# One mixing step for three head groups in the first layer of a decode kernel

## The chip, the core and the metric

The kernel runs on one core of a Trainium2 chip. The metric is the device time of one execution in microseconds; the figure for a kernel is the median of its runs. Beside those times there is one profiled execution, whose trace gives the span (first to last instruction) and every instruction and transfer in it.

## The reference

Two layers, the same weights and caches in both. Each layer is an attention block over a cached sequence of 8192 positions, for one new position in each of 4 batches, followed by a gated feed-forward block; both have a layer norm before them and are added to x.

```python
def A(x, k_cache, v_cache, wq, wo):        # x: 4 x 1 x 512, caches: 4 x 8 x 8192 x 128
    q = (x @ wq).reshape(B, Sq, 32, 128).transpose(0, 2, 1, 3)
    k, v = repeat(k_cache, 4, axis=1), repeat(v_cache, 4, axis=1)
    p = softmax(einsum("bhqd,bhkd->bhqk", q, k) * 128 ** -0.5)
    o = einsum("bhqk,bhkd->bhqd", p, v)
    return o.transpose(0, 2, 1, 3).reshape(B, Sq, 4096) @ wo
def B(x, w_gate, w_up, w_down):            # 512 -> 1792 -> 512
    return (silu(x @ w_gate) * (x @ w_up)) @ w_down
x = x + A(layernorm(x), ...)
x = x + B(layernorm(x), ...)
x = x + A(layernorm(x), ...)
x = x + B(layernorm(x), ...)
```

All tensors are bfloat16. The two caches are 268 MB together if each were read once for each layer (part of what layer 1 has loaded last is kept for layer 2).

## The kernel before, in words

**Units and groups.** The 8 key/value heads make 4 groups `gp` of two heads, each group with 8 query heads (`H2`). With 4 batches there are 16 units `u` = 4 gp + b. A unit has one K block and one V block of 4 MB (4096 KB, 128 partitions x 32 KB). In the text, K13 and V13 are the blocks of unit 13. Layer 1 (`L` = 0 in the code) goes through the groups in the order 0, 1, 2, 3, layer 2 through 3, 0, 1, 2.

**Slots and transfers.** Blocks lie in four slots of one large tile `kvf`, and a fifth place that wq holds at first. All loads are issued by SyncE (SP) in one order that the program writes out (`cmds`). Each waits until the room that it writes is free; `freed` marks a room free, and `pump` issues whatever can then be issued, in order. After the last V blocks of layer 1 come the weights of the feed-forward block: gate and up into the slot of V13, then two parts of `w_down`, and then three more parts of `w_down`, each written over a quarter of the gate weights as soon as the products with that quarter (line 1016) have read it. Behind them come K blocks of layer 2, each into room that the feed-forward block gives back.

**One unit.** VectorE (DVE) transposes the K block in place (`turn`, line 567), two of its eight parts at a time. TensorE (PE) makes the scores from each part (`scores`, line 593, four products of 512 columns for a part). Then come a maximum (lines 599, 604, 607), the exponential on ScalarE (ACT, line 641), a transpose of the weights p (`turn_p`, line 659), the products with V (line 731, 16 for each half), the gathering of the heads' outputs out of PSUM on DVE (`gather`, lines 779 and 783), and a small product with `sel` and a scaling (`combine`, lines 788 and 793) that put the unit's eight heads into the tile `oT`.

**The end of a group.** When the four batches of a group are done, `close_group` queues what follows. `mix` (line 815) rearranges the group's columns of `oT` by 16 small products into PSUM and one copy back (line 819), since `w_o` was loaded with four rows beside one another on a partition. `rows` (line 850) then makes 8 products for the group, each with 4 columns of `oT` as weights and 512 columns of `w_o` moving; all groups but the last add up in one PSUM bank. When the last but one group of a layer is in, `upright` turns the 4 x 512 sum into the layout of x: four times a copy on ACT (line 864) and a small transpose on PE (line 860), and then an addition to x on DVE (line 804). The last group goes another way (`out_proj`, line 875), directly in the layout of x.

**What sets the order.** The instruction order of each engine is fixed when the program is built. Score and value work is held in a list `blocks`, each with 0.9 us; small steps stand in a list `line`, each with the time that should pass before it. Running a block advances `line` by the block's time, and due steps are emitted. `flush` empties `line` at once. It is called, among other places, in `finished` (line 536), when part 6 of K13 in layer 1 is done:

```python
if it == half_kept and a >= NB - 2:
    flush()
    hold(a, False)
```

`hold` (line 533) transposes the last two of the eight parts of K13 into PSUM, to keep them for layer 2; after that the slot of K13 is free. A second list, `later`, holds work for the end of the next unit's values.

In layer 1 the mixing of groups 0 and 1 is done when group 1 closes (`spot` gives a group's place in its layer's order), with their rows at the end of the next unit; group 2 is mixed and added when it closes. In layer 2 the first three groups are mixed together when the third closes.

Of the kernel before, what the change touches and what calls it, by code (L numbers as in the profile page):

```python
# [103 lines left out]
def bass_interleave_layers__gqa_block_cached__swiglu_ffn__decode_kernel(  # L104
# [40 lines left out]
    with ExitStack() as es:  # L145
# [35 lines left out]
        def pick2(k):  # L181
            o = k // 2 * 2 * P + k % 2
            return slice(o, o + 2 * P - 1, 2)
# [69 lines left out]
        n = FO * B  # L253
# [24 lines left out]
        def bank(k):  # L278
            return ps[:, k * BANKF:(k + 1) * BANKF]
# [75 lines left out]
        groups = [[0, 1, 2, 3], [3, 0, 1, 2]]  # L355

        def spot(L, gp):
            return groups[L].index(gp)
# [51 lines left out]
        n = NB - PARK  # L410
# [140 lines left out]
        line = []  # L551
# [162 lines left out]
        def values(L, u):  # L714
# [22 lines left out]
            def part(i):  # L737
# [18 lines left out]
                if i == 3:  # L756
                    more = later.pop(0)() if later else []
                    if p_name == "late":
                        freed(W_SLOT[L], NB, NB + 1)
                    if (L, u) == (0, NP - 2):  # L760
                        freed(W_SLOT[L], NB + 1, NB + 2)
                    done.add((L, u))
                    if last:
                        gather([QH - 1], ok3)
                        combine()
                    else:
                        line[0:0] = [[0.0, None, lambda: gather(range(QH), ok, True)], [1.3, None, combine]]
                    line.extend(behind.pop(u, []))
                    if all((L, gp * B + k) in done for k in range(B)):
                        close_group(L, gp, fill)  # L770
                    line.extend(more)
# [31 lines left out]
        def add_to_x(at, name):  # L803
            T.op("dve", lambda e: e.tensor_tensor(xT[:], xT[:], at, ALU.add), reads=["x", name], writes=["x"])  # L804

        def mix(L, gs, fill):
            C = len(gs) * H2 // NA
            mixed.update(gs)
            at, name = place("mix", 0, NA * C * B)
            names = [OT[g] for g in gs]  # L810
            now = oT[:, spot(L, gs[0]) * H2:(spot(L, gs[-1]) + 1) * H2]
            o = now.rearrange("p (c a) b -> p a c b", a=NA)
            for j in range(NA):
                for a in range(NA):
                    T.op("pe", lambda e: e.matmul(at[a * QB:(a + 1) * QB, j * C * B:(j + 1) * C * B],
                                                  lhsT=ident[:, j::NA], rhs=o[:, a], start=True, stop=True),
                         reads=["ident"] + names, writes=[name], sig=(j == NA - 1 and a == NA - 1))
            fill(1)
            T.op("dve", lambda e: e.tensor_copy(now.rearrange("p (c j) b -> p j c b", j=NA),  # L819
                                                at.rearrange("p (j c b) -> p j c b", j=NA, c=C)),  # L820
                 reads=[name], writes=names)

        mixed, later = set(), []

        def close_group(L, gp, fill):
            if gp == groups[L][-1]:
                line.extend([[0.5, None, lambda: mix(L, [gp], fill)], [0.7, None, lambda: out_proj(L, gp, fill)]])
                return
            n = spot(L, gp)
            if n < (1, 2)[L]:  # L830
                return
            gs = groups[L][:n + 1] if n == (1, 2)[L] else [gp]
            line.append([0.5, None, lambda: mix(L, gs, fill)])
            turned_back = upright() if gp == groups[L][-2] else []

            def in_rows():
                while gp not in mixed:
                    line.pop(0)[2]()
                for g in gs:
                    rows(L, g)  # L840
                return turned_back
            if turned_back and not L:
                line.extend([[0.7, None, in_rows]] + turned_back)
            else:
                later.append(in_rows)

        def rows(L, gp):
            for r in range(H2):
                h, o = gp * H2 + r, spot(L, gp) * H2 + r
                T.op("pe", lambda e: e.matmul(bank(OUTB)[0:B, 0:D], lhsT=oT[:, o, :], rhs=wo_sb[:, h, :],  # L850
                                              start=(gp == groups[L][0] and r == 0),
                                              stop=(gp == groups[L][GP - 2] and r == H2 - 1)),
                     reads=[f"wo{gp}", OT[gp]], writes=[f"pb{OUTB}"], sig=(r == H2 - 1))

        def upright():
            at, name = bank(LNB)[:, 4 * P - XB:4 * P], f"pb{LNB}"

            def step(kt):
                if kt:
                    T.op("pe", lambda e: e.matmul(at[:, (kt - 1) * B:kt * B], lhsT=row, rhs=identf[0:B, 0:B],  # L860
                                                  is_transpose=True, start=True, stop=True),
                         reads=["row", "ident"], writes=[name])
                if kt < KT:
                    T.op("act", lambda e: e.activation(row, bank(OUTB)[0:B, pick2(kt)], ACTF.Copy),
                         reads=[f"pb{OUTB}"], writes=["row", "pb"])
                else:
                    add_to_x(at, name)
            return [[0.9, None, lambda kt=kt: step(kt)] for kt in range(KT + 1)]
# [11 lines left out]
        def out_proj(L, gp, fill):  # L880
            project(L, gp)
            fill(1)
            add_to_x(*place("out", 0, XB))
# [268 lines left out]
```

## Time and profile before

| | |
|---|---|
| median of 3 runs | 644.83 us (644.80 to 645.44) |
| the profiled execution | 645.2 us, its span 642.9 us |
| busy: PE, PE weight loads, DVE, ACT | 413.0, 173.2, 424.9, 50.2 us |
| moved | 271.8 MB, mean 423 GB/s |
| row products (line 850) | 48 of them, 10.8 us busy |
| mixing products (line 815) | 80 of them, 1.2 us busy |
| mean granted clock of PE | 0.834 |

How to read it: the share of busy time is an average over the whole span. In the trace a line of the timeline gives start, length, engine, line of the code, operation, output and input, the number of instructions, and in brackets how long the engine was idle before and what ended that. Lines with SPq are issues of transfers, not the transfers. A line of the windows gives, for a stretch of the span, its length, the busy time and the number of instructions of PE, PE's weight loads, DVE, ACT and POOL, then PE's granted clock (1.00 is full speed), the share of the 16 DMA engines that was busy, and GB/s. A clock of 0.50 is half speed.

### The profile page before, as it was taken

To read this page: it belongs to the slowest core of one execution; us is meant where nothing else is said; L and a number is where in the kernel's file an instruction comes from. 1 tells how busy PE (TensorE), PEld (TensorE's weight loads), DVE (VectorE), ACT (ScalarE), POOL (GpSimd) and SP (SyncE) were. 2 spreads that over 40 slices of the span, in tenths; PEclk is the share of its full clock that TensorE was granted. 3 is DMA by queue.
4 is the path that set the end of the run, shared out by engine and by line. 5 is a ranking of instruction groups with operands and counts; after the bars stand their busy time and mean duration, and the time that the engine had idled before them with its cause. 6 is when DMAs were issued, how large, how long until landed. Compare 5 with 4: busy or idle time off the path is not lost.

```text
span 642.9 us, 6981 instructions
## 1 busy us (share of the span) xinstructions
PE 413.0 (64%) x2886; PEld 173.2 (27%) x2888; DVE 424.9 (66%) x597; ACT 50.2 (8%) x138; POOL 11.9 (2%) x44
## 2 busy tenths in 40 slices
PE   0583476457755757757866977667655477558766
PEld 0231122122222312222325332222222122223224
DVE  5375467456776656776953888977765567656953
ACT  0100000000000000000010300000000000000110
POOL 0000000000000000000000000000000000000000
PEclk9995886688876898768975899998767987679987
DMA  9999999999999999999999999999999999999996
GB/s 365 451 423 414 436 430 432 433 428 423 436 438 427 426 432 433 433 430 429 428 414 386 416 435 431 433 431 429 434 428 430 435 430 432 424 436 429 431 414 261
DMA packets 16014, 271.76 MB, mean 423 GB/s; under 512 B 1640, under 2 KB 1648, under 8 KB 7536
## 3 DMA queue, kind: packets, MB, share of 16 engines
q1 hardware_dynamic: 15984, 271.33, 99.1%
q8 instruction: 22, 0.36, 0.2%
q14 instruction: 8, 0.07, 0.0%
HBM read 271.32 MB, written 0.00 MB: 422 GB/s over the span
## 4 chain that ended last, share of the span: by engine, by line
DMA 60%; DVE 19%; PE 16%; issue 4%; ACT 0%; SPq 0%; POOL 0%; ACTq 0%; DVEq 0%; POOLq 0%
DMA kvf<-in_A_k_cache_dram 45%; DVE kvf L567 14%; DMA kvf<-in_A_v_cache_dram 11%; PE ps L593 10%; DMA kvf<-in_A_wq_dram 3%; PE ps L731 2%; DVE pb L783 2%; DMA kvf<-in_B_w_down_dram 1%; PE ps L982 1%; PE ps L1016 1%; DVE pT L659 1%; DVE pb L779 0%; DVE ps L533 0%; DVE scr L793 0%; PE ps L875 0%
## 5 line engine op out<-in xcount | busy, mean ns | idle before, releaser
L593 PE MATMUL ps<-kvf,zq 128*128 128x512 bf16 x1024 | 291.8, 431 | 185.6 <-DVE kvf L567 178.6
L567 DVE STREAM_TRANSPOSE kvf<-kvf 128x2048 f32<-128x2048 f32 (+1 forms) x133 | 280.5, 2132 | 125.5 <-DMA kvf<-in_A_k_cache_dram 125.3
L593 PEld LDWEIGHTS ps<-kvf,zq 128*128 128x128 bf16 x1024 | 98.9, 108 | 343.1 <-DVE kvf L567 222.6
L731 PE MATMUL ps<-kvf,pT 128*32 128x512 bf16 x960 | 65.8, 396 | 1.4 <-DVE pT L659 1.4
L641 ACT ACTIVATE pb<-ps,tiny 128x512 bf16<-128x512 f32 x32 | 24.9, 777 | 507.8 <-DVE tiny L639 507.8
L659 DVE STREAM_TRANSPOSE pT<-pb 64x512 bf16<-64x512 bf16 x60 | 41.2, 686 | 3.0 <-ACT pb L641 2.0
L783 DVE SCALAR_TENSOR_TENSOR pb<-ps,tiny,pb 128x128 f32<-128x128 f32 x104 | 36.5, 351 | 5.1 <-PE ps L731 1.4
L599 DVE TENSOR_REDUCE tiny<-ps 128x1 f32<-128x512 f32 x32 | 22.0, 688 | 20.5 <-PE ps L593 20.5
L731 PEld LDWEIGHTS ps<-kvf,pT 128*32 128x32 bf16 x960 | 20.8, 98 | 31.1 <-issue 15.4
L788 PEld LDWEIGHTS ps<-sel,pb 128*128 128x128 f32 x64 | 16.5, 266 | 16.4 <-DVE pb L783 8.0
L583 POOL TENSOR_TENSOR zq<-scr,tiny 128x64 bf16<-128x64 bf16 x30 | 9.2, 307 | 525.9 <-PE ps L593 525.9
L607 DVE TENSOR_REDUCE mrm<-ps 1x8 f32<-1x128 f32 x32 | 8.7, 273 | 13.5 <-PE ps L604 13.5
L788 PE MATMUL ps<-sel,pb 128*128 128x8 f32 x64 | 12.1, 262 | 5.4 <-DVE pb L783 5.4
L631 PEld LDWEIGHTS ps<-mrm,tiny 128*128 128x128 f32 x60 | 13.0, 223 | 9.3 <-issue 5.9
L982 PE MATMUL ps<-kvf,xn 128*4 128x512 bf16 x64 | 7.5, 621 | 11.2 <-DMA kvf<-in_A_wq_dram 10.9
L631 PE MATMUL ps<-mrm,tiny 128*128 128x16 f32 x60 | 10.0, 243 | 3.3 <-ACT mrm L644 3.3
L779 DVE TENSOR_SCALAR pb<-ps,tiny 128x128 f32<-128x128 f32 x32 | 10.1, 316 | 2.6 <-PE ps L731 2.6
L850 PE MATMUL ps<-wo_sb,scr 128*4 128x512 bf16 x48 | 10.8, 379 | 0.4 <-DVE scr L819 0.4
L644 ACT ACTIVATE mrm<-head,tiny 128x8 f32<-128x8 f32 x32 | 9.6, 301 | 1.0
L604 PE MATMUL ps<-identf,tiny 128*1 128x128 f32 x32 | 8.6, 270 | 1.2 <-DVE tiny L599 1.2
L804 DVE TENSOR_TENSOR xT<-xT,ps 128x16 f32<-128x16 f32 x6 | 1.0, 172 | 10.6 <-PE ps L860 4.7
L793 DVE TENSOR_TENSOR scr<-ps,rl 128x8 bf16<-128x8 f32 x32 | 5.7, 177 | 3.1 <-PE ps L788 2.1
(88 smaller groups left out, 122.6 us busy)
## 6 DMA issues: line engine op xcount, KB each, us to landing
kvf<-in_A_k_cache_dram SPq DMA_DIRECT2D x27, 4096.0 KB, 31.2
kvf<-in_A_v_cache_dram SPq DMA_DIRECT2D x27, 4096.0 KB, 33.8
kvf<-in_A_v_cache_dram SPq DMA_DIRECT2D x3, 2048.0 KB, 25.0
kvf<-in_A_k_cache_dram SPq DMA_DIRECT2D x11, 512.0 KB, 6.9
kvf<-in_A_k_cache_dram SPq DMA_DIRECT2D x2, 2048.0 KB, 9.4
kvf<-in_A_wq_dram SPq DMA_DIRECT2D x2, 2048.0 KB, 18.1
wo_sb<-in_A_wo_dram SPq DMA_DIRECT2D x4, 1024.0 KB, 41.5
kvf<-in_B_w_gate_dram SPq DMA_DIRECT2D x2, 1792.0 KB, 24.0
```

What stands on the lines that cost most here:

```text
L567: T.op("dve", lambda e: e.transpose(w, w), reads=names, writes=names)
L593: T.op("pe", lambda e: e.matmul(bank(bk)[:, 0:SW], lhsT=zq[:, z0:z0 + P], rhs=w[:, :, c // 2, :, c % 2], start=(q == 0 and c == 0), stop=( ...
L599: T.op("dve", lambda e: e.tensor_reduce(mx[:], bank(bk)[:, 0:SW], AX.X, ALU.max), reads=[f"pb{bk}"], writes=["mx"])
L631: T.op("pe", lambda e: e.matmul(at, lhsT=ones, rhs=mrm[:, i * H2:(i + 2) * H2], start=True, stop=True), reads=[f"m8{i}", "rsm", "onesf"], ...
L641: T.op("act", lambda e: e.activation(pb[:], bank(bk)[:, 0:SW], ACTF.Exp, bias=nm, scale=rstd[:, b:b + 1], accum_out=rs), reads=[f"pb{bk}", ...
L659: T.op("dve", lambda e: e.transpose(dst, pb[hp]), reads=["pb", "row"], writes=[name])
L731: T.op("pe", lambda e: e.matmul(bank(k)[j * QB:(j + 1) * QB, q0 * Dh:q1 * Dh], lhsT=p_t[:, t, h, :], rhs=v[:, q0:q1, t, :], start=((last o ...
L779: T.op("dve", lambda e: e.tensor_scalar(into, o, own[:, q:q + 1], None, op0=ALU.mult), reads=[f"pb{k}", "own"], writes=["row"] if last els ...
L783: T.op("dve", lambda e: e.scalar_tensor_tensor(into, o, own[:, q:q + 1], into, op0=ALU.mult, op1=ALU.add), reads=[f"pb{k}", "own", iname], ...
L788: T.op("pe", lambda e: e.matmul(at, lhsT=into, rhs=sel[:], start=True, stop=True), reads=[iname, "sel"], writes=[name])
L850: T.op("pe", lambda e: e.matmul(bank(OUTB)[0:B, 0:D], lhsT=oT[:, o, :], rhs=wo_sb[:, h, :], start=(gp == groups[L][0] and r == 0), stop=(g ...
L982: T.op("pe", lambda e: e.matmul(bank(QK[k])[a * QB:a * QB + B, :], lhsT=xn[:, kt * B:(kt + 1) * B], rhs=wq_sb[:, kt, f:f + W2], start=(kt ...
```

## The change

In layer 1, `close_group` now does nothing when groups 0 and 1 close. When group 2 closes, one `mix` takes the 24 heads of groups 0, 1 and 2 together: 16 small products of 24 columns instead of 16 of 16 columns and 16 of 8, and one copy instead of two. The 8 row products of each of the three groups are put into `line` as three steps with times of 0.7, 1.8 and 1.8 us, followed by the steps of `upright`. The number of row products is the same, 24 in each layer. Layer 2 is as before.

```diff
@@ close_group
             if gp == groups[L][-1]:
                 line.extend([[0.5, None, lambda: mix(L, [gp], fill)], [0.7, None, lambda: out_proj(L, gp, fill)]])
                 return
-            n = spot(L, gp)
-            if n < (1, 2)[L]:
+            if gp != groups[L][-2]:
                 return
-            gs = groups[L][:n + 1] if n == (1, 2)[L] else [gp]
+            gs = groups[L][:-1]
             line.append([0.5, None, lambda: mix(L, gs, fill)])
-            turned_back = upright() if gp == groups[L][-2] else []
+            turned_back = upright()
 
             def in_rows():
                 while gp not in mixed:
...
                 for g in gs:
                     rows(L, g)
                 return turned_back
-            if turned_back and not L:
-                line.extend([[0.7, None, in_rows]] + turned_back)
-            else:
+            if L:
                 later.append(in_rows)
+            else:
+                line.extend([[0.7 if g == gs[0] else 1.8, None, lambda g=g: rows(L, g)] for g in gs] + turned_back)
```

## The prediction

> **What bounds the kernel now.** I read the page first. Its part 2 says that the transfers never rest:
>
> ```profile
> DMA  9999999999999999999999999999999999999996
> GB/s 365 451 423 414 436 430 432 433 428 423 436 438 427 426 432 433 433 430 429 428 414 386 416 435 431 433 431 429 434 428 430 435 430 432 424 436 429 431 414 261
> ```
>
> The second line counts. 271.3 MB at the usual 431 GB/s is 629 us of a 642.9 us span. One place in the middle is slow: slice 22 (337.5 to 353.6 us), with 386 GB/s. It loses 16.07 x (1 - 386/431) = 1.7 us. It is the feed-forward part of the first layer, so I asked for SP's own timeline there:
>
> ```profile
> 296.97 14.30 SPq L93 DMA_DIRECT2D kvf<-in_A_v_cache_dram  x5
> 323.57 0.38 SPq L93 DMA_DIRECT2D kvf<-in_B_w_gate_dram  x1
> 324.00 2.14 SPq L93 DMA_DIRECT2D kvf<-in_B_w_up_dram  x3
> 338.42 0.33 SPq L93 DMA_DIRECT2D kvf<-in_B_w_down_dram  x1
> 338.80 0.41 SPq L93 DMA_DIRECT2D pT<-in_B_w_down_dram  x1
> 343.31 1.61 SPq L93 DMA_DIRECT2D kvf<-in_B_w_down_dram  x3
> ```
>
> The reader is to see how much is queued ahead of each issue. From 296.97 to 323.57 a loss is impossible: at 296.97 the last K block (4.19 MB, 9.7 us) is still to come, and at 323.57 some 5 MB of V are (11.5 us, bytes issued less bytes of the packets ended). At 343.31 it is different. The last V packets end at 334.7 us; behind them are only gate 1.835, up 1.835 and two quarter-megabyte parts of down, together 4.19 MB. At the 409 to 410 GB/s of 338 to 342 us they last 10.2 us, until 344.9. The next issue, 343.31, waits until the first gate products (L1016) have read the room it overwrites, and packets follow an issue by a little over 1 us here (the first issue is at 0.74, the first packets are in the stretch 1.5 to 2.0). So the queue is on the edge, and the windows of half a microsecond show it:
>
> ```profile
> 343.00:343.50 0.50, 0.50 (x22) 0.50 (x20) 0.01 (x1) 0.00 (x0) 0.00 (x0) 0.50 1.08 399
> 343.50:344.00 0.50, 0.50 (x11) 0.50 (x9) 0.00 (x0) 0.00 (x0) 0.00 (x0) 0.50 0.72 279
> 344.00:344.50 0.50, 0.50 (x20) 0.50 (x20) 0.00 (x0) 0.35 (x2) 0.00 (x0) 0.50 0.89 295
> 344.50:345.00 0.50, 0.50 (x22) 0.50 (x20) 0.03 (x1) 0.21 (x1) 0.00 (x0) 0.50 0.91 266
> ```
>
> The last two columns are the DMA share and GB/s: 280 in the mean of the last three lines against 410, so some 0.5 us is lost already. The slack here is nil. Whatever makes the first gate product later makes this hole longer, and the hole is not made good, because the DMA engines are busy from there to 639 us.
>
> **The change, part by part.** Units are (group, batch); K13 is the K block of unit 13.
>
> *Taken away at 210 and 214 us* (group 1 closes): 16 mixing products of 0.42 us together, one copy of 0.22 us (L819, 211.85), and 16 row products that take 3.62 us from 214.53. After them PE waits 3.46 us for the transpose of a K block, itself waiting for its DMA at 219.24. The transfer issued at 212.62, just behind the mixing, comes up to 0.42 us earlier, with 15 us queued ahead of it. Gain at the end: nothing, and covered so deeply that no bound is needed.
>
> *One mix of three groups instead of one group.* Layer 2 of this kernel already does just this: 16 products of 24 columns in 0.42 us (580.74), the same as the 16 of 8 columns at 288.45, and its copy takes 0.26 instead of 0.19. Cost +0.07 us.
>
> *The rows moved.* The list gives the three sets of rows due times of 0.7, 1.8 and 1.8, which looks like a spreading. The order of the changed kernel's instructions shows none: on PE all 24 row products stand in one block, just where the 8 stand now. The reason is in `finished`: when quarter 6 of K13's eight parts is done, `flush()` empties the whole list before `hold` puts the last parts of K13 into PSUM. In the trace this is the place:
>
> ```profile
> 288.45 0.42 PE L815 MATMUL ps<-scr,identf 128*32 128x8 bf16 x16
> 289.91 0.19 DVE L819 CAST scr<-ps 128x32 bf16<-128x32 f32 x1
> 290.25 1.89 PE L850 MATMUL ps<-wo_sb,scr 128*4 128x512 bf16 x8 [0.40 <-DVE scr L819]
> 294.48 0.17 DVE L804 TENSOR_TENSOR xT<-xT,ps 128x16 f32<-128x16 f32 x1 [4.38 <-PE ps L860]
> 298.07 2.29 DVE L567 STREAM_TRANSPOSE kvf<-kvf 128x2048 f32<-128x2048 f32 x1
> ```
>
> After the rows come four copies on ACT and four small products on PE in turn (L864, L860), the add to x, the two transposes of `hold`, a maximum, and only then K14's first transpose. DVE sits idle 4.38 us in this already and is in order, so K14's transposes stand behind it; so do the last quarter of K13 and V12 on PE. The price of the 24 rows is in layer 2, at the same granted clock of 1.0:
>
> ```profile
> 585.38 5.34 PE L850 MATMUL ps<-wo_sb,scr 128*4 128x512 bf16 x24
> ```
>
> 5.34 - 1.89 = 3.45 us more, 3.5 with the copy. Nothing covers it: from K13's arrival (277.64) on, the compute side is the late one. K14's last packets end at 296.1, its transposes start at 298.07, now at 301.6; K15's end at 305.9, its transposes start at 310.3, now 313.8. Between 298.1 and 310.3 DVE is busy 11.93 of 12.20 us, so it cannot catch up. The chain view puts "DMA 25.89 us" from 310.12 here, the last V parts; that is queueing behind V13 and V14, and an issue 3.5 us later still finds 16 us ahead of it.
>
> *Where the delay meets the first wait that takes some of it.* The last V block:
>
> ```profile
> 336.06 0.83 PE L731 MATMUL ps<-kvf 128*32 128x384 bf16 x16 [1.30 <-DMA kvf<-in_A_v_cache_dram]
> 336.95 1.58 DVE L783 SCALAR_TENSOR_TENSOR pb<-ps,tiny,pb 128x128 f32<-128x128 f32 x4 [0.57 <-PE ps L731]
> 337.30 0.62 PE L731 MATMUL ps<-kvf 128*32 128x128 bf16 x16 [0.41 <-DMA kvf<-in_A_v_cache_dram]
> ```
>
> PE has 1.30 us to spare. DVE has only 0.57: before these four it gathers V14 and the first half of V15, each 1.5 us, and it is DVE's last gather that releases the combining product (338.58), the last mix, the projection, the norm and the gate. So 0.57 is absorbed and 3.5 - 0.57 = 2.9 us arrive at the gate products: 342.66 becomes 345.6, and the issue at 343.31 becomes 346.2. The weights for `up`, gate and the first parts of `down` were issued early and do not shift. So the hole in the queue grows by about 2.9 us. Later issues are shifted by no more than that (the product at 346.34 waits 0.56 us for `up` and then needs not), so no second hole opens, and layer 2 runs as now with all of it later.
>
> **Bounds of this sum.** Low: if PE's spare 1.30 us and the 0.56 us at 346.34 were both usable, 3.5 - 1.9 = 1.6. High: nothing absorbed and the restart of a queue that is truly empty slower, as at the start of the span, where the half microseconds from 1.5 to 3.5 move 360, 164, 33 and 492 GB/s, 0.52 MB instead of 0.86: 0.8 us more, and with the unabsorbed 3.5 it makes 4.3. I take 2.9, since the trace shows the DVE row as the tight one. The profiled execution took 645.2 us for a span of 642.9; 645.8 and 648.1 with the change. The median of before is 644.83, so 647.7.
>
> **The clock.** PE's granted clock alternates between 1.0 and 0.5: mean 1.00 from 288.5 to 298.1 and 0.72 from 298.1 to 310.3. The 128x512 score products take 0.45 us apiece in the slow stretches (8 in 3.60 at 280.01) and about 0.24 in the fast ones (8 in 1.91 at 592.51). At the slow pace 24 rows would be some 10.5 us instead of 5.34. The Trainium skill, "TensorE: Matmul & The Clock Gate", Part 1, says that the clock is halved after an idle window of about 3.4 us and given back by a busy one; by it the moved rows, in the middle of busy PE work, run at full clock and the sum stays at 2.9. Layer 2's row at 585.38 agrees.
>
> **Rivals.**
> 1. *It is hidden.* DMA is 99% busy and 9 to 20 us are queued until 323 us, so a late PE would matter to nobody. For it: every issue up to 324.00. Against it: the 0.72 share at 343.50. It needs over 2.2 us absorbed before the gate product, for instance if K14 and K15 run faster where the clock returns earlier (PE 10.54 of 12.20 us busy there, but DVE 11.93). Then +0 to +1.2: 644.8 to 646.0. Chance 0.15.
> 2. *The clock drops in or after the longer burst.* One further slow stretch of 3.4 us on the bound path doubles about 1.7 us of products: +4.6, 649.4; in the rows themselves up to +8. For it: the slow stretch that now begins at 299.5 would fall on work already late. Against: DVE, not PE, is the tight engine there. Chance 0.18.
> 3. *Faster.* The work removed at 210 to 218 us changes when PE's clock is granted, and the last chain (326 to 344, mean clock 0.5 to 0.7 over most of it) runs at full clock. It gains only from the point where the gate products come over 2.9 us earlier than the sum has them; the whole loss of slice 22 is 1.7 us, so the least time is 643.1. Chance 0.03.
> 4. *The change does not cluster the rows*: excluded by the instruction order.
>
> The forecast has the remaining 0.64. The range 645.6 to 649.6 takes in the bounds 1.6 and 4.3, rival 2's ordinary size and the upper end of rival 1. A measurement of this kernel can tell about 0.2% (1.3 us) from no change. Faster is rival 3, 0.03; within 0.2% is rival 1, 0.15; the rest is slower, 0.82.
>
> **What would show it.** In the changed profile: 24 row products of about 5.3 us near 290, K14's first transpose near 301.6, the waits on DMA at 336.06 and 337.30 gone, the third `down` issue near 346.2, and a hole of about 3 us in the DMA share before its packets; slice 22 falls from 386 to some 310 GB/s and slices after 23 stay as they are. If the gate products are late and no hole is there, or K14 starts where it does now, I am wrong about the queue or the cover.

## The result: 0.27% slower

The changed kernel takes 646.92 us (median of 9 runs, 646.34 to 647.37) against 645.31 us (9 runs on the same chip, 644.36 to 645.83). The ratio is 1.0027, with a 95% interval of 1.0016 to 1.0037: 1.7 us more, between 1.0 and 2.4. The profiled execution took 646.6 us with a span of 644.7, against 645.2 and 642.9.

The page of the changed kernel, its transfers in 40 slices:

```profile
DMA  9999999999999999999998999999999999999996
GB/s 371 442 422 418 448 424 431 422 425 440 435 425 432 436 430 423 433 439 428 425 415 333 412 435 436 429 424 434 435 428 427 436 431 429 426 441 426 429 416 268
```

Slice 22 has fallen from 386 to 333 GB/s, and the DMA row, which was 9 everywhere up to the last slice, has its one 8 there. The other slices differ from the kernel before by at most 17 GB/s, in both directions. SP's timeline and the windows of half a microsecond in the changed kernel show the place (the last two columns of the windows are DMA share and GB/s):

```profile
300.10 14.12 SPq L93 DMA_DIRECT2D kvf<-in_A_v_cache_dram  x5
338.81 0.33 SPq L93 DMA_DIRECT2D kvf<-in_B_w_down_dram  x1
339.20 0.41 SPq L93 DMA_DIRECT2D pT<-in_B_w_down_dram  x1
345.19 1.88 SPq L93 DMA_DIRECT2D kvf<-in_B_w_down_dram  x3
```

```profile
344.50:345.00 0.50, 0.45 (x15) 0.48 (x16) 0.36 (x2) 0.00 (x0) 0.00 (x0) 0.50 0.64 250
345.00:345.50 0.50, 0.50 (x20) 0.50 (x16) 0.00 (x0) 0.00 (x0) 0.00 (x0) 0.50 0.36 115
345.50:346.00 0.50, 0.50 (x10) 0.50 (x9) 0.00 (x0) 0.00 (x0) 0.00 (x0) 0.50 0.14 53
346.00:346.50 0.50, 0.50 (x21) 0.50 (x19) 0.00 (x0) 0.46 (x2) 0.00 (x0) 0.50 0.72 184
```

The third issue of `w_down`, which waits for the first gate products, comes at 345.19 instead of 343.31. Around it the queue runs dry, to 53 GB/s in the half microsecond from 345.5, and the restart is ragged until 348.5. The same 16 us of both kernels, before and then after:

```profile
338.00:354.00 16.00, 10.63 (x236) 8.93 (x240) 4.44 (x23) 0.82 (x3) 0.00 (x0) 0.50 1.01 385
```

```profile
338.00:354.00 16.00, 9.23 (x244) 8.34 (x236) 5.72 (x25) 0.81 (x3) 0.00 (x0) 0.61 0.87 331
```

The difference, 54 GB/s for 16 us, is 0.86 MB, and at 431 GB/s that is 2.0 us of transfers. The span is 1.8 us longer. So nearly all of the time went into this one hole.

The start of the delay, in the timeline of the changed kernel:

```profile
287.47 0.42 PE L815 MATMUL ps<-scr,identf 128*32 128x24 bf16 x16
289.52 0.26 DVE L819 CAST scr<-ps 128x96 bf16<-128x96 f32 x1
289.93 5.34 PE L849 MATMUL ps<-wo_sb,scr 128*4 128x512 bf16 x24 [0.66 <-DVE scr L819]
297.61 0.17 DVE L804 TENSOR_TENSOR xT<-xT,ps 128x16 f32<-128x16 f32 x1 [7.83 <-PE ps L859]
301.20 2.29 DVE L567 STREAM_TRANSPOSE kvf<-kvf 128x2048 f32<-128x2048 f32 x1
```

The mix of three groups takes 0.42 us, its copy 0.26, the 24 rows 5.34, all as layer 2 had them. DVE waits 7.83 us instead of 4.38 for the addition to x, and K14's first transpose is 3.13 us later.

### The profile page after: what moved, and what is told of

It reads as the page before. It is cut to its first block, busy times and chain, and to the rows that moved or that the text cites. A ratio compares the mean times of both kernels' runs of the same rounds, so it can differ in the third digit from the quotient of the medians.

```text
span 644.7 us, 6948 instructions
## 1 busy us (share of the span) xinstructions
PE 410.4 (64%) x2870; PEld 171.8 (27%) x2872; DVE 424.4 (66%) x596; ACT 50.2 (8%) x138; POOL 11.8 (2%) x44
## 4 chain that ended last, share of the span: by engine, by line
DMA 57%; DVE 23%; PE 14%; issue 4%; ACT 0%; SPq 0%; ACTq 0%; DVEq 0%
DMA kvf<-in_A_k_cache_dram 46%; DVE kvf L567 17%; DMA kvf<-in_A_v_cache_dram 7%; PE ps L593 7%; DMA kvf<-in_A_wq_dram 3%; PE ps L731 3%; DVE pb L783 2%; PE ps L981 1%; DMA kvf<-in_B_w_down_dram 1%; PE ps L849 1%; DVE pT L659 1%; PE ps L1015 1%; DVE pb L779 1%; DVE scr L793 0%; DVE ps L533 0%
## 5 line engine op out<-in xcount | busy, mean ns | idle before, releaser
L788 PEld LDWEIGHTS ps<-sel,pb 128*128 128x128 f32 x64 | 15.9, 256 | 17.6 <-DVE pb L783 9.7
L788 PE MATMUL ps<-sel,pb 128*128 128x8 f32 x64 | 11.7, 255 | 7.1 <-DVE pb L783 7.1
L941 DVE STREAM_TRANSPOSE ps<-ps 128x512 f32<-128x512 f32 x4 | 2.9, 721 | 7.5 <-PE ps L981 7.4
```

What stands on the lines that cost most here:

```text
L788: T.op("pe", lambda e: e.matmul(at, lhsT=into, rhs=sel[:], start=True, stop=True), reads=[iname, "sel"], writes=[name])
```

## The experiments

Every ratio below is to the kernel before on the same chip, with its 95% interval; "third issue" is the third issue of `w_down`. In the edits, `...` marks lines left out, and added products are written without the helper through which the kernels issue them. Three accounts compete in the first four. H: the rows moved in front of the addition to x delay the first gate products, and the hole grows. E: what costs is the work missing at 210 to 218 us. M: what costs is the larger mix.

**late16: the delay alone, in the kernel before.**

```diff
 def rows(L, gp):
+    if not L and gp == groups[L][-2]:
+        for _ in range(16):   # 4 columns of wo_sb as weights, 512 moving, into bank TOT
+            matmul(bank(TOT)[0:B, 0:D], lhsT=wo_sb[:, 0, 0:B], rhs=wo_sb[:, 0, :])
```

> The kernel before, with 16 extra products of 4x128 by 128x512 (results unused) on PE just ahead of group 2's rows near 290 us; mixing and rows of groups 0 and 1 stay where they were. Theory H (the later first gate products lengthen the hole in the transfers): as with the change, +1.2 to +2.4 us, K14's first transpose about 3.4 us later and the hole at 344 to 349 us. Rival E (what costs is that PE's work at 210 to 218 us is gone): 0, within 0.5 us. Rival M (the mix of three and its copy cost): 0, within 0.5 us.

Measured: ratio 1.0038 (1.0026 to 1.0051), +2.5 us. K14's first transpose at 300.88, 2.8 us later (the extra products need not wait for the copy and start 0.8 us before the rows would), third issue at 345.26, 122 GB/s in the window 345 to 347 us. The time lies just above the expected +1.2 to +2.4. The delay alone brings the loss; the mix and the early part are untouched here. So neither E nor M is needed for it.

**after_early16: the early work put back into the changed kernel.**

```diff
 if gp != groups[L][-2]:
+    if not L and gp == groups[L][1]:
+        later.append(lambda: idle_products(16) or [])
     return
```

> The changed kernel with 16 products (results unused) put back on PE at 214 us, where the rows of groups 0 and 1 were. H: as the change, +1.2 to +2.4 us. E: back to the kernel before, within 0.5 us. M: as the change.

`idle_products(16)` puts in the 16 products of late16. Measured: 1.0024 (1.0014 to 1.0035), third issue at 345.70; the 16 products run from 214.25 us, for 3.62 us as the rows there did. The loss stays, so it does not come from what is missing at 214 us. This run does not tell H from M.

**before_wo3 and after_wo3: slack instead of delay.** The last megabyte of `w_o` is loaded behind the last V block, so that everything between arrives some 2.4 us earlier by its size (K13's first transpose came 2.8 us earlier in before_wo3, at 274.87), with the same bytes ahead of the hole.

```diff
-for n, i in ((4, 0), (7, 1), (10, 2), (13, 3)):
+for n, i in ((4, 0), (7, 1), (10, 2)):
     cmds.insert(n, (("wo", i), None, 0, 0))
 ...
-cmds += [(("W", 0), W_SLOT[0], 0, PARK),
+cmds += [(("wo", 3), None, 0, 0), (("W", 0), W_SLOT[0], 0, PARK),
```

> The kernel before, with the load of the last quarter of w_o (1 MB) moved from behind the seventh block (near 71 us) to just behind the last V block of layer 1. The bytes ahead of the hole are the same, but each K and V block from there on arrives 2.4 us earlier. H: the issue after the gate products comes some 2 us earlier, the hole near 344 us is gone, -0.3 to -0.9 us. Rivals, by which the transfers have no hole that matters: 0, within 0.2 us.

> The changed kernel with the same move of the last quarter of w_o. H: the 1.9 us of delay fit into the 2.4 us won, so the change costs at most 0.5 us against the same move without the change: -0.8 to +0.2 us against the kernel before. Rivals (E, M, or the later issue of V13 at 300 us): the loss stays, 1.2 us or more above the same move without the change.

Measured: before_wo3 0.9994 (0.9985 to 1.0003), after_wo3 0.9991 (0.9982 to 1.0000), their third issues at 342.35 and 343.21. With the slack there, the change costs nothing that can be told (645.14 against 645.25 us): that is the strongest evidence for H, and it clears E and M too, which have no reason to vanish with this move. It also clears the later issue of V13, which comes at 297.65 in after_wo3 and at 294.19 in before_wo3, still 3.46 us apart. That before_wo3 itself wins something cannot be told from its interval. Its third issue is only 0.96 us earlier, not 2, because another wait takes over, in its timeline:

```profile
341.68 1.01 PE L1016 MATMUL ps<-xn,kvf 128*128 128x4 bf16 x28 [1.96 <-DMA kvf<-in_B_w_gate_dram]
```

The gate products now wait 1.96 us for the gate weights to land. That limit does not move, since the bytes ahead of it are the same.

**late8 and late32: the dose.** The same extra products as in late16, 8 and 32 of them.

> The kernel before with 8 extra products (results unused) on PE ahead of group 2's rows near 290 us, half the dose of late16. With 16 the addition to x came 2.7 us later and 1.3 us later at the gate products than without absorbing would be. H with its slack: 1.0 us later at the addition to x, nearly all of it absorbed by DVE's 0.5 us and the quicker clock: 0 to +0.5 us. A cost in proportion (no slack): half of late16, +1.2 us.

> The kernel before with 32 such products. H with its slack: 6.1 us later at the addition to x, 1.2 us absorbed, +4.3 to +5.6 us. A cost in proportion to late16's: +4.9 us. A loss that is capped, since later waits on the transfers would take up what is late: +2 to +3 us.

Measured: late8 0.9996 (0.9987 to 1.0005), third issue 343.46; late32 1.0083 (1.0069 to 1.0097), +5.4 us, third issue 348.35. Eight products cost nothing that can be told, where a cost in proportion would be +1.2 us, and sixteen cost 2.5: there is slack and then a price of about one for one, as H has it. The slack lies ahead of the issue: of late8's 0.81 us at K14's first transpose 0.15 are left at the third issue, of late32's 6.32 there are 5.04. The loss of late32 is not capped; on its own it would also fit a cost in proportion to late16's.

**project: an earlier addition to x.** Rows of groups 0 and 1 are summed and turned upright after group 1; group 2 goes the way of group 3.

```diff
-gs = groups[L][:n + 1] if n == (1, 2)[L] else [gp]
+if not L and n == 2:
+    line.extend([[0.5, None, lambda: mix(L, [gp], fill)], [0.7, None, lambda: out_proj(L, gp, fill)]])
+    return
+gs = groups[L][:n + 1]
 ...
-turned_back = upright() if gp == groups[L][-2] else []
+turned_back = upright()
 ...
-if turned_back and not L:
 ...
-else:
-    later.append(in_rows)
+later.append(in_rows)
 ...
-            stop=(gp == groups[L][GP - 2] and r == H2 - 1)
+            stop=(gp == groups[L][(1, GP - 2)[L]] and r == H2 - 1)
```

> The other way round: in layer 1 the rows of groups 0 and 1 are summed and turned upright after group 1, near 220 us, where PE waits for transfers, and group 2 is projected directly in the layout of x (32 products of 128x128 by 128x4), as group 3 is. The addition to x near 294 us comes 2 to 3 us earlier. H: nothing is won beyond the last V block's landing, the gate products come 0 to 0.6 us earlier: -0.5 to +0.2 us. A cost in proportion (each microsecond at 290 us is a microsecond at the end): -2 us or better.

Measured: 1.0017 (1.0008 to 1.0026), +1.1 us. This was a miss. In its timeline:

```profile
291.00 0.17 DVE L804 TENSOR_TENSOR xT<-xT,ps 128x16 f32<-128x16 f32 x1 [1.13 <-PE ps L875]
297.03 2.31 DVE L567 STREAM_TRANSPOSE kvf<-kvf 128x2048 f32<-128x2048 f32 x1 [2.36 <-DMA kvf<-in_A_k_cache_dram]
335.96 1.90 PE L731 MATMUL ps<-kvf 128*32 128x384 bf16 x32 [2.33 <-DMA kvf<-in_A_v_cache_dram]
337.48 1.58 DVE L783 SCALAR_TENSOR_TENSOR pb<-ps,tiny,pb 128x128 f32<-128x128 f32 x4 [2.24 <-PE ps L731]
343.84 1.57 SPq L93 DMA_DIRECT2D kvf<-in_B_w_down_dram  x3
```

The addition to x comes 3.5 us earlier, K14 then waits for its own landing, and PE waits 2.33 instead of 1.30 us for the last V parts. The expectation had this right. The last 32 V products end where they did (337.86 and 337.92 us), but the first 16 of them, which DVE's last gathers wait for, take longer: the gathers start at 337.48 instead of 336.95, and these 0.53 us are what the third issue comes later. The granted clock goes with it: in the windows of this kernel it is 0.50 from 334.5 to 337.5 us, where the kernel before has 0.93:

```profile
331.00:334.50 3.50, 1.81 (x26) 0.63 (x18) 2.18 (x7) 0.00 (x0) 0.00 (x0) 0.99 0.98 406
334.50:337.50 3.00, 1.54 (x28) 0.76 (x32) 0.72 (x3) 0.00 (x0) 0.00 (x0) 0.50 1.03 421
```

PE was busy for only 1.81 of the 3.50 us ahead. The Trainium skill, "TensorE: Matmul & The Clock Gate", Part 1, says that an idle window of about 3.4 us halves the clock. The clock stretches in these traces are multiples of 3.41 us (in the kernel before 6.8 us at half speed from 299.5 and from 326.9 us, 20.5 us from 337.1), which agrees; how much idleness counts, no run here shows. Nor is it shown that the longer wait halved the clock here: project_warm runs the same instructions up to 334 us, and there the clock stayed at 0.50 from 326.3 to 336.5 us, where in `project` it was at 1.00 from 331.1 to 334.5.

The late issue does not account for the whole loss either. From 338 to 354 us `project` moves 376 GB/s against 385 of the kernel before, which is 0.3 us of transfers; another 0.4 us are lost from 360 to 364 us, at 373 GB/s against 415. Why, no run here shows.

**project_wo3: the same with w_o moved.**

> The same, with the last quarter of w_o loaded behind the last V block of layer 1. H: the gate weights' landing is what the first gate products wait for, as with that move alone (1.96 us there), so no more than with it: -0.7 to +0.1 us. In proportion: -2 us or better.

Measured: 1.0007 (0.9998 to 1.0016), third issue 342.18; the gate products wait 1.30 us for their weights. It is no better than before_wo3, as H has it, though the +0.5 us lie above the expected range, into which only the interval reaches.

**project_warm and before_warm: holding the clock in the wait.**

```diff
 gather(range(QH), ok, True)
 fill(3)
+for _ in range(0 if L else 8):   # 5 in before_warm
+    matmul(bank(ok2)[:, 0:D], lhsT=wo_sb[:, 0, 0:P], rhs=wo_sb[:, 0, :])
```

> The kernel 'project' with 8 more products of 128x128 by 128x512 on PE (results unused, written to the bank that the next products start afresh) in its 2.3 us wait for the last V parts of layer 1. Theory C (in 'project' the longer wait halves PE's clock from 334.5 us on, the last V products take 1.9 instead of 1.5 us and the gate products come 0.5 us later): the clock stays at 1.0 through the last V products, the gate products come at least 0.5 us earlier than in 'project', near 342.7 us, and the time is -0.6 to +0.5 us against the kernel before instead of +1.1. Rival (the upright steps put between group 2's work near 231 us cost it): stays at +0.7 to +1.5 us.

> The kernel before with 5 such products in its 1.3 us wait at the same place. C: the half-speed stretch from 337.1 us on begins at least 3.4 us later, the chain from the last V products to the first gate product, 5.4 us now at half speed, becomes 0.2 to 0.5 us shorter, as in the changed kernel: -0.6 to 0 us. Rival (the clock does not matter there): 0, or +0.2 to +0.6 us where the five products delay the last V products.

Measured: project_warm 1.0013 (1.0002 to 1.0023), third issue 344.20; before_warm 0.9995 (0.9986 to 1.0004), third issue 343.09. What C expected of project_warm did not come: its third issue is 0.36 us later than that of `project`. It decides nothing, since in its profile the clock was already at half when the eight products came (2.76 us in the first line below), and they held up the last V products until 337.41. In before_warm the clock stays at 1.00 until 341 us. The last gathers end no earlier for it; the gain lies behind them, in the combining products, which start where they did and take 0.39 us where the kernel before needs 0.59 (second and third line; L791 there is L788 in the kernel before). The third issue is 0.22 us earlier, too little to see in the time.

```profile
334.72 2.76 PE L748 MATMUL ps<-wo_sb 128*128 128x512 bf16 x8
```

```profile
338.61 0.39 PE L791 MATMUL ps<-sel,pb 128*128 128x8 f32 x2 [0.86 <-DVE pb L786]
```

```profile
338.58 0.59 PE L788 MATMUL ps<-sel,pb 128*128 128x8 f32 x2 [0.66 <-DVE pb L783]
```

All kernels together, in the order of the third issue; issue and span are those of the profiled execution, the difference comes from the ratio of all runs:

| kernel | third issue, us | span, us | against before, us |
|---|---|---|---|
| project_wo3 | 342.18 | 642.8 | +0.5 |
| before_wo3 | 342.35 | 642.9 | -0.4 |
| before_warm | 343.09 | 642.9 | -0.3 |
| after_wo3 | 343.21 | 642.8 | -0.6 |
| before | 343.31 | 642.9 | |
| late8 | 343.46 | 642.5 | -0.3 |
| project | 343.84 | 643.8 | +1.1 |
| project_warm | 344.20 | 644.3 | +0.8 |
| after | 345.19 | 644.7 | +1.7 |
| late16 | 345.26 | 645.3 | +2.5 |
| after_early16 | 345.70 | 645.4 | +1.5 |
| late32 | 348.35 | 648.9 | +5.4 |

Up to about 343.5 us the issue time is worth nothing that can be told, with intervals of some 0.6 us either way. After that each microsecond costs about one. The kernel before stands near the bend; the single spans say less than the last column, since that of the kernel before lay between 642.2 and 645.3 us in the runs beside the experiments. None of the versions tried beats it by more than the measurement can tell.

## Why the prediction was right, and where its size was off

- **The early part costs and gains nothing.** Right: after_early16 loses as much with the early products put back.
- **24 rows for 5.34 us, with the price from layer 2's row, and no spreading.** Right to the hundredth, and in one block. Rival 2, a clock that drops in the rows, did not come.
- **Nothing covers it between 290 and 323 us.** Nearly right. From K13's arrival (0.20 us earlier in this execution) to K14's first transpose the delay is 3.33 us, against 3.5, or 3.13 by the time in the span; of these 3.13, at V13's products (324.19 instead of 321.25) 2.94 are left.
- **The hole at the third issue and no second one.** Right, shown by the windows, by after_wo3 and by the table. The waits at 336.06 and 337.30 are gone, as foretold. It is not so that the issues of the weights do not shift: gate goes from 323.57 to 326.51 and `down` from 338.42 to 338.81. These found transfers queued ahead of them and cost nothing.
- **0.57 us absorbed.** This term was mis-sized. Of the 3.13 us at K14's first transpose, 1.88 reach the third issue: 1.25 are absorbed. DVE's idle time before the last gathers gives 0.47 of the 0.57 forecast (the combining product L788 goes from 2.57 us late to 2.10). The rest, 0.78, is what the sum left out, and is in pieces: 0.19 up to V13's products, 0.33 between V14's and V15's products, 0.04 up to V14's combining, 0.22 from the last combining to the issue. Each is a stretch of products whose clock is now higher. For the first piece, the stretch in which the kernel before has K14's first products, before and then after (which is about 3 us behind, so that other work stands in it):

```profile
298.10:304.00 5.90, 4.29 (x26) 1.62 (x14) 5.79 (x8) 0.00 (x0) 0.00 (x0) 0.62 0.99 428
```

```profile
298.10:304.00 5.90, 3.12 (x39) 0.96 (x37) 5.50 (x7) 0.00 (x0) 0.30 (x1) 1.00 1.02 439
```

  The granted clock is 1.00 instead of 0.62 there, and K14's first eight score products take 1.91 us at 303.55 instead of 3.59 at 300.42. It is also 1.00 instead of 0.50 from 337.5 to 341.0 us, where the last combining product takes

```profile
340.68 0.39 PE L788 MATMUL ps<-sel,pb 128*128 128x8 f32 x2 [2.37 <-DVE pb L783]
```

  instead of 0.59 us. The forecast had no term for the clock in its sum: it could cost in rival 2 and help in rivals 1 and 3, with chances of 0.15 and 0.03. It gave back up to 0.8 us. That the clock is the cause of these pieces is read from the traces. before_warm, which holds it up at the last place, shows the 0.22 us there. Of the 0.33 some may be another wait: in the kernel before the weights for V15's first products are shown to be loaded only when its V has landed,

```profile
332.37 0.33 PEld L731 LDWEIGHTS ps<-kvf 128*32 128x32 bf16 x8 [0.52 <-DMA kvf<-in_A_v_cache_dram]
```

  so that at full clock these products could have started only 0.17 us earlier there, not 0.33. Nor is the amount the same each time: between K14's first transpose and the third issue late8 loses 0.66 us of its delay, late16 0.86, after_early16 0.90 and late32 1.28, against 1.25 here.
- **The forecast and the rivals.** 2.9 us were forecast and 1.7 measured (1.0 to 2.4), near the low bound of 1.6; slice 22 fell to 333 GB/s, not to some 310. That bound had been set from other terms (PE's 1.30 us and the wait for `up`), so that it fits is partly luck. Rival 1, hidden, needed more than 2.2 us absorbed, and 1.25 were; with a delay a quarter as long (late8) it is what happens. Rival 3's idea, that earlier gate products close a hole and win up to 1.7 us, is not borne out: before_wo3 issues 0.96 us earlier with no win that can be told, so slice 22's 386 GB/s is mostly not a hole (before_wo3 has 386 there too). Nor is the half microsecond that the prediction calls lost already shown to be one: with the earlier issue 370 instead of 310 GB/s move from 343 to 345 us, and yet 387 instead of 385 from 338 to 354.

## What to carry to other kernels

In a kernel whose transfers are always busy, look for the one place where the queue's backlog is shorter than the compute chain that releases the next issue; a microsecond before it is free or costs a microsecond, according to which side of that bend the kernel stands. Moving work out of idle time into a chain that is already late is paid there even if the instruction count falls, and due times in an emission list spread nothing if something empties the list first. When the slack is sized, ask also what the moved work does to the clock.

## What was not expected of the hardware

- Being earlier can end later: in `project` PE's work ended 3.5 us earlier at 291 us, the last V parts landed only 0.1 us earlier, the clock was at 0.50 when they came, and DVE's last gathers started 0.53 us later than in the kernel before. Whether the longer wait brought the clock down stays open.
- Busy share alone does not tell the clock: from 298.1 to 304.0 us the kernel before had PE busy for 4.29 of 5.90 us at a mean clock of 0.62, the changed one, with other work in that stretch, for 3.12 at 1.00. Slow products are busy for longer: the same eight take 3.59 us at half clock and 1.91 at full.
- A queue that has run dry does not come back at once. In the changed kernel the DMA share is 0.36 and 0.14 in the microsecond from 345.0 to 346.0, around the issue at 345.19. By 347.07 the three issues of `w_down` from 345.19 on are out, 1.3 MB together, but from 345.5 to 348.0 only 156 GB/s are moved, 0.39 MB, where the kernel before has 369 GB/s. No run here shows what holds them back.
